# Full-width loads, one index load, one transpose of the token weights, and fillers moved to the known waits, in an attention and MLP kernel

## The chip, the cores and the metric

The kernel runs on 1 core of one Trainium2 chip. The metric is the device time of one execution in microseconds (us), the slowest core's, and with one core that is the only one. The kernel before took 499.61 us in the median of 3 runs (498.57 to 500.69).

## The reference, cut to what matters

Eight batches, each with 8 heads of 576 rows and head width 64, go through attention with a band of 32 rows to either side and 8 global rows and columns. An MLP block over 512 channels follows, which first mixes the 576 tokens with a 576x576 matrix.

```python
def _attn_ref(q, k, v, global_idx):               # (8, 8, 576, 64) each
    scores = scale * np.matmul(q, k.transpose(0, 1, 3, 2))
    mask = np.abs(pos[:, None] - pos[None, :]) <= 32
    mask = mask | is_global[:, None] | is_global[None, :]
    # ... softmax over the masked scores, then:
    return np.matmul(attn, v)

def _moe_ref(x, alpha1, beta1, w_tok, alpha2, beta2, w_ch1, w_ch2, lam):   # x is (8, 576, 512)
    a1 = alpha1 * x + beta1
    tok = np.einsum('ts,bsd->btd', w_tok, a1)     # token mixing
    u = x + lam * tok
    a2 = alpha2 * u + beta2
    ch = np.maximum(a2 @ w_ch1, 0.0) @ w_ch2      # the two large MLP matmuls
    return u + lam * ch
```

## The kernel before

The MLP matmuls of finished batches are a stock of independent work for TensorE. `front(b)` emits the attention and the token mixing of batch b and is a Python generator. Each `yield n` in it means "put n MLP matmuls here". These are the fillers: they keep TensorE busy while another engine prepares what attention needs next. There are none during batch 0, because the MLP has nothing to work on yet.

```python
for b in range(NB):
    for n in front(b):
        for _ in range(n):
            if b > 0:
                next(fill)                     # one MLP matmul of an earlier group
```

The loading phase, cut. `A(tile, offset, dims)` is an access pattern. `V`, `SC`, `G`, `T` are VectorE, ScalarE, GpSimd (POOL in the profile) and TensorE (PE). `nc.sync` is the queue of SyncE (SP).

```python
gbc_i = cp.tile([P, 8], I32, name="gbc_i")       # the global index on every partition: 128 x 8 pieces of 4 bytes
nc.scalar.dma_start(out=gbc_i, in_=bass.AP(gi32.tensor, gi32.offset, [[0, P], [2, 8]]))
# ... three more tiny loads of the same index
R = [cp.tile([P, 1536], FP32, name=f"R{i}") for i in range(3)]      # staging buffers

def load_qk(b):
    for hh in range(2):                           # k on 96 partitions, runs of 1536 bytes
        r = next_r()
        nc.sync.dma_start(out=A(r, 0, [[384, 4], [1, 384]], 0, PK), in_=k[b, 4 * hh : 4 * hh + 4, :, :].rearrange("h (p c) d -> p h (c d)", c=NK))
        (V if b == 0 else G).tensor_copy(...)     # cast to bf16
    for h0, nh in ((0, 3), (3, 3), (6, 2)):       # q on 72 partitions, runs of 2048 bytes
        ...
def load_v(b):
    ...                                           # v to ve, cast by POOL; vo is ve shifted by 64 rows:
    nc.sync.dma_start(out=A(vo, 0, [[1, 2080]], 0, 64), in_=A(ve, 0, [[1, 2080]], 64, 64))
    nc.sync.dma_start(out=A(vo, 0, [[1, 2080]], 64, 64), in_=A(ve, 520, [[1, 2080]], 0, 64))
```

One batch, cut to what the argument needs:

```python
def front(b):
    ...                                           # kqn: the gathered global rows of k and q, made by POOL
    for p in range(4):                            # four pairs of heads
        # 6 TensorE transposes of k; two VectorE copies of 64 x 576 from PSUM to KTz
        # 8 TensorE transposes of q; one ScalarE copy to QT
        # after p == 0: transpose of kqn, copies to KgT and QT
        yield 4
    ...
    def qk(p):                                    # scores of a head pair: 3 groups of 6 matmuls
        ...
        SC.activation(out=Pt[...], in_=ps[:, 0:432], func=AF.Exp, bias=0.0, scale=0.125)
        yield 4                                   # after each group
        ...                                       # VectorE makes GRT and PTz from Pt

    def pv(p):
        ...                                       # global rows: 10 matmuls on GRT, then VectorE copies to RS
        yield 4
        # values: matmuls of PTz with ve or vo, and one of RS for each block; VectorE makes x
        # POOL makes XL from x, the input of token mixing

    ...                                           # global scores: QT with KgT
    yield from qk(0)
    for p in range(4):
        if p < 3:
            yield from qk(p + 1)
        else:
            yield 4
        yield from pv(p)
    ...
    yield 14
    ...                                           # token mixing: 5 blocks of 5 matmuls on XL, yield 4 after each
```

KTz and QT hold the transposed k and q. kqn holds the gathered global rows of k and q, and KgT those of k, transposed. RS is what the global rows add to the values. LA1 is the product of alpha1 and lam, by which POOL scales x into XL. PSUM is the memory that TensorE writes into.

In the fillers' stream, `wt_prep(1)` stands before the first MLP matmul. It is a second preparation of the token weights (25 TensorE transposes, 10 small matmuls, the copies), for the odd batches, whose rows are shifted by 64.

The softmax here doesn't subtract the row's maximum and nothing guards it: scores larger than these inputs give would overflow.

## Time and profile before

I use the first global-score matmul of each batch, which reads `KgT`, as the mark between batches. It divides the 496.3 us of the profiled execution into five stages.

| stage (us from the start) | length | TensorE busy | idle |
|---|---|---|---|
| start to KgT of batch 0 (43.17) | 43.17 | 4.79 | 38.38 |
| to KgT of batch 1 (102.44) | 59.27 | 41.96 | 17.31 |
| batch 1 (to 152.83) | 50.39 | 45.89 | 4.50 |
| batches 2 to 6 (to 393.92) | 241.09 | 226.97 | 14.12 |
| batch 7 and the MLP tail (to 496.3) | 102.38 | 97.02 | 5.36 |

These are the lines behind it, the stage view of the kernel before. The columns are: window, length, then busy time and (number) of PE, PEld (weight loads), DVE (VectorE), ACT (ScalarE) and POOL, the granted clock of TensorE, the mean busy share of the DMA engines, and GB/s.

```profile
0.00:43.17 43.17, 4.79 (x57) 3.96 (x58) 20.38 (x61) 8.32 (x9) 25.60 (x35) 1.00 0.62 132
43.17:102.44 59.27, 41.96 (x486) 28.77 (x484) 39.12 (x76) 20.13 (x34) 34.66 (x37) 0.74 0.82 227
102.44:152.83 50.39, 45.89 (x465) 26.44 (x464) 26.64 (x54) 22.18 (x40) 24.05 (x25) 1.00 0.73 159
152.83:393.92 241.09, 226.97 (x2296) 130.56 (x2295) 127.17 (x263) 107.23 (x192) 88.83 (x93) 1.00 0.38 96
393.92:496.30 102.38, 97.02 (x648) 47.36 (x646) 25.05 (x51) 40.05 (x65) 6.88 (x8) 1.00 0.09 32
```

The first stage loads, TensorE hardly works in it, and the DMA engines are busy for only 0.62 of it. So neither limits it: something waits. In the second stage the clock column reads 0.74. TensorE had half its clock for three stretches of 10.24 us, 30.7 us in all. From 102 us on TensorE is nearly full, and its idle time is the question. The waits view names it. First the loading: the wait of the sync queue, then two lines of the queue's timeline (start, length, engine, line, what is issued).

```profile
SPq L167 <- DMA gbc_i<-in_global_idx_dram: 13.8, 1, 13.8
```

```profile
1.17 0.47 SPq L158 DMA_DIRECT2D R_102<-in_k_dram  x1
15.50 0.35 SPq L167 DMA_DIRECT2D R_103<-in_q_dram  x1
```

The queue issues k by 1.6 us and then stands still for 13.8 us before q. What it waits for is the landing of the index, in 1,024 pieces of 4 bytes. Later on TensorE waits for kqn, and POOL, which makes it, is held up by other work. The timeline of POOL in the kernel before, with the idle time before an instruction and its releaser in brackets:

```profile
25.20 1.26 POOL L503 TENSOR_TENSOR LA_240<-U,lamb 128x512 f32<-128x512 f32 x1 [9.16 <-DMA U<-in_moe_alpha_dram]
26.40 2.23 POOL L505 MEMSET XL_136<- 128x2560 bf16 x1
28.57 2.23 POOL L505 MEMSET XL_137<- 128x2560 bf16 x1
...
37.61 0.38 POOL L301 CAST kqn<-kq 64x128 bf16<-64x128 f32 x1
```

For the steady state, the waits of TensorE in the window of batches 2 to 6 alone, 152.83 to 393.92 us (total, times, longest):

```profile
PE sc L462 <- POOL XL_137 L412: 3.4, 2, 1.7
PE sc L462 <- POOL XL_136 L406: 2.6, 3, 0.9
PE xps L395 <- DVE RS_134 L382: 2.2, 6, 0.4
PE mm L316 <- DVE UT L452: 2.0, 5, 0.6
PE mm L316 <- DVE QT L324: 1.8, 3, 0.6
PE xps L395 <- DVE RS_133 L382: 1.1, 4, 0.6
```

Token mixing waits for XL: 6.0 us in five batches. The values wait for RS: 3.3 us. The transposes (L316) wait 3.8 us for VectorE to free a PSUM buffer. These 13.1 us are nearly all of the stage's 14.12 us of idle time.

### The profile page before, as it was taken

The numbers are of one execution on the slowest core, as the hardware profiler recorded it, in microseconds if no ns is written. First come the engines' busy times: TensorE is split into PE (matmuls) and PEld (weight loads), VectorE is DVE, ScalarE is ACT, GpSimd is POOL, SyncE is SP. The second block draws the span as 40 slices with busy tenths as digits, with TensorE's granted clock in tenths as the row PEclk, the third lists the DMA queues.
The fourth block names the chain that finished last, engine by engine and source line by source line (L and its number), as shares of the span: only waits on it lengthen the run. The fifth ranks groups of instructions, "written<-read, shape, count | busy, mean of one in ns | idle before, by whom it ended". The sixth has DMA issues, their size and how long they took to land. (4 is left out here: it accounts for less than half of the span.)

```text
span 496.3 us, 9426 instructions
## 1 busy us (share of the span) xinstructions
PE 416.6 (84%) x3942; PEld 237.1 (48%) x3942; DVE 238.4 (48%) x501; ACT 197.9 (40%) x337; POOL 180.0 (36%) x196
## 2 busy tenths in 40 slices
PE   0006767798899999998999999989999999999996
PEld 0004643455455555654556455545564555444442
DVE  4615756745464557353735472547354645501101
ACT  0225602185039503840384148214831581262440
POOL 4296495346606262426232543343233013000000
PEclk9999669699999999999999999999999999999999
DMA  4687767989766153706270645063103000101102
GB/s 95 160 153 200 259 167 231 222 198 191 164 146 150 45 136 92 190 4 163 66 187 20 151 108 143 24 143 86 35 22 87 23 1 22 44 21 42 44 5 81
DMA packets 62946, 53.60 MB, mean 108 GB/s; under 512 B 42088, under 2 KB 48616, under 8 KB 62904
## 3 DMA queue, kind: packets, MB, share of 16 engines
q1 hardware_dynamic: 59248, 51.73, 40.7%
q10 hardware_dynamic: 2888, 0.88, 0.9%
q0 software_dynamic: 768, 0.39, 0.4%
q8 instruction: 31, 0.51, 0.4%
q14 instruction: 11, 0.09, 0.1%
HBM read 39.30 MB, written 9.44 MB: 98 GB/s over the span
## 5 line engine op out<-in xcount | busy, mean ns | idle before, releaser
L485 PE MATMUL ml<-UT,W_139 128*128 128x512 bf16 x576 | 146.8, 379 | 0.0
L494 PE MATMUL ml<-W_140,HTb 128*128 128x512 bf16 x576 | 140.2, 379 | 0.0
L488 ACT ACTIVATE HTb<-ml,bias1T 128x512 bf16<-128x512 f32 x144 | 99.0, 687 | 43.0 <-PE ml L485 42.8
L494 PEld LDWEIGHTS <-HTb 128*128 128x128 bf16 x576 | 53.0, 98 | 55.6 <-issue 0.2
L485 PEld LDWEIGHTS <-W_139 128*128 128x128 bf16 x576 | 49.2, 98 | 41.8 <-issue 3.6
L351 ACT ACTIVATE Pt<-sc 128x432 f16<-128x432 f32 x96 | 50.4, 529 | 29.1 <-DVE rden L397 18.0
L498 DVE TENSOR_TENSOR U<-ml,U 128x512 f32<-128x512 f32 x36 | 24.9, 691 | 60.1 <-PE ml L494 59.8
L463 DVE TENSOR_TENSOR U<-sc,x 128x512 f32<-128x512 f32 (+1 forms) x40 | 27.6, 690 | 45.4 <-PE sc L462 45.4
L406 POOL TENSOR_TENSOR XL_137<-x,LA_240 128x512 bf16<-128x512 f32 x16 | 20.3, 1266 | 71.9 <-DVE x L399 71.9
L317 ACT COPY QT<-mm 128x576 bf16<-128x576 bf16 x32 | 20.4, 638 | 38.9 <-PE mm L316 38.9
L406 POOL TENSOR_TENSOR XL_136<-x,LA_240 128x512 bf16<-128x512 f32 x16 | 20.3, 1266 | 38.8 <-DVE x L399 38.7
L462 PE MATMUL sc<-XL_136,wtT_142 128*128 128x512 bf16 x100 | 26.1, 395 | 4.3 <-POOL XL_136 L406 4.3
L316 PE MATMUL mm<-identb,q_114 72*128 72x72 bf16 x256 | 14.5, 204 | 17.9 <-ACT q_114 L173 11.1
L462 PE MATMUL sc<-XL_137,wtT_143 128*128 128x512 bf16 x100 | 24.8, 379 | 5.3 <-POOL XL_137 L412 5.3
L399 DVE TENSOR_TENSOR x<-xps,rden 128x640 f32<-128x640 f32 x32 | 26.3, 823 | 1.4
L353 DVE TENSOR_TENSOR GRT_129<-Pt,grm 128x80 f16<-128x80 f16 x16 | 4.4, 277 | 42.6 <-ACT Pt L351 42.6
L308 PE MATMUL mm<-identb,k_115 96*128 96x96 bf16 x192 | 14.3, 214 | 11.0 <-DVE k_115 L162 9.5
L316 PEld LDWEIGHTS <-q_114 72*128 72x128 bf16 x256 | 12.5, 102 | 21.5 <-ACT q_114 L173 11.3
L300 POOL TENSOR_TENSOR kqn<-kq,cst 64x128 bf16<-64x128 f32 x8 | 3.2, 394 | 50.8 <-PE mm L321 50.8
L394 PEld LDWEIGHTS <-PTz_128 128*128 128x128 f16 x288 | 15.7, 100 | 10.4 <-issue 4.8
L394 PEld LDWEIGHTS <-PTz_127 128*128 128x128 f16 x288 | 15.8, 99 | 10.3 <-issue 7.9
L395 PE MATMUL xps<-RS_134,GS_132 128*128 128x65 f16 x160 | 15.7, 193 | 5.7 <-DVE RS_134 L382 5.4
(272 smaller groups left out, 698.5 us busy)
## 6 DMA issues: line engine op xcount, KB each, us to landing
out_dram<-U SPq DMA_DIRECT2D x36, 256.0 KB, 2.0
vo<-ve SPq DMA_DIRECT2D x16, 260.0 KB, 4.1
RV_105<-in_v_dram SPq DMA_DIRECT2D x16, 256.0 KB
R_101<-in_k_dram SPq DMA_DIRECT2D x6, 576.0 KB, 7.8
R_102<-in_k_dram SPq DMA_DIRECT2D x5, 576.0 KB, 5.7
R_103<-in_k_dram SPq DMA_DIRECT2D x5, 576.0 KB
R_103<-in_q_dram SPq DMA_DIRECT2D x6, 432.0 KB
R_101<-in_q_dram SPq DMA_DIRECT2D x5, 432.0 KB
```

The lines of the kernel that those rows point to most:

```text
L316: T.transpose(out=ps[:, c * PQ : (c + 1) * PQ], in_=q16[0:PQ, c, p * P : (p + 1) * P], identity=identb[0:PQ, 0:PQ])
L317: SC.copy(out=A(QT, 648 * p, [[72, 9], [8, 8], [1, 8]]), in_=A(ps, 0, [[8, 9], [1, 8], [PQ, 8]]))
L351: SC.activation(out=Pt[:, 432 * un : 432 * un + 432], in_=ps[:, 0:432], func=AF.Exp, bias=0.0, scale=0.125)
L394: T.matmul(out=o_, lhsT=ptz[:, base : base + P], rhs=vv, start=(i == 0), stop=False)
L399: V.tensor_tensor(out=A(x, P * p, [[64, 2], [DM, 5], [1, 64]]), in0=A(xps, 0, [[512, 2], [65, 5], [1, 64]]), in1=A(rden, 0, [[5, 2], [1, 5 ...
L406: G.tensor_tensor(out=A(xl, DM * full + P * p, [[DM, 4], [1, P]]), in0=A(x, DM * full + P * p, [[DM, 4], [1, P]]), in1=A(LA1, P * p, [[0, ...
L462: T.matmul(out=ps, lhsT=wtT[par][:, c, P * u : P * u + P], rhs=xl[:, c, :], start=(c == 0), stop=(c == 4))
L463: V.tensor_tensor(out=U[f][r0:r1, :], in0=ps[r0:r1, :], in1=x[r0:r1, u, :], op=ALU.add)
L485: T.matmul(out=ps, lhsT=W1[:, cc, ec * P : (ec + 1) * P], rhs=ut[:, cc, :], start=(cc == 0), stop=(cc == 3))
L488: SC.activation(out=HTb[:, slots[ec], :], in_=ps, func=AF.Relu, bias=bias1T[:, ec : ec + 1], scale=1.0)
L494: T.matmul(out=ps, lhsT=HTb[:, slots[ec], P * j : P * j + P], rhs=W2[:, ec, :], start=(ec == 0), stop=(ec == 15))
L498: V.tensor_tensor(out=u, in0=ps, in1=u, op=ALU.add)
```

## The change

Its intent has four parts.

1. **Loading.** The index comes in one load of 64-byte pieces and nothing slow stands ahead of q. k and q come on all 128 partitions in runs of 1 KB (rows 0 to 511), with a tail load of rows 512 to 575. POOL's memsets and LA1 are cut or moved.
2. **Transposes.** With 128 rows at a time, a head pair takes 4 + 4 transposes instead of 6 + 8, and the tails take 8 for all pairs: 41 a batch instead of 57, with the one for kqn.
3. **Token weights.** They are prepared once, and the odd batches' copy is made from it by two DMAs. The vo copies move from the sync queue to POOL's.
4. **Fillers.** They move from where nothing waits to where TensorE was seen waiting: before token mixing and between the global rows and the values.

```diff
-    R = [cp.tile([P, 1536], FP32, name=f"R{i}") for i in range(3)]
+    R = [cp.tile([P, 1024], FP32, name=f"R{i}") for i in range(4)]
...
-        nc.scalar.dma_start(out=gbc_i, in_=bass.AP(gi32.tensor, gi32.offset, [[0, P], [2, 8]]))
+    nc.scalar.dma_start(out=gi_t, in_=bass.AP(gi32.tensor, gi32.offset, [[0, P], [1, 16]]))
...
+        for i, src in enumerate((k, q)):
+            for hh in range(2):
+                r = next_r()
+                nc.sync.dma_start(
+                    out=A(r, 0, [[256, 4], [1, 256]]),
+                    in_=src[b, 4 * hh : 4 * hh + 4, 0:512, :].rearrange("h (p c) d -> p h (c d)", c=4),
+                )
...
-        nc.sync.dma_start(out=A(vo, 0, [[1, 2080]], 0, 64), in_=A(ve, 0, [[1, 2080]], 64, 64))
+        G.dma_start(out=A(vo, 0, [[1, 2080]], 0, 64), in_=A(ve, 0, [[1, 2080]], 64, 64))
... (the second vo copy likewise; the index arithmetic, now behind the first casts on VectorE)
-            for c in range(NK):
-                T.transpose(out=ps[:, c * PK : (c + 1) * PK], in_=k16[0:PK, c, p * P : (p + 1) * P], ...)
+            for c in range(4):
+                T.transpose(out=ps[:, c * P : (c + 1) * P], in_=kq16[:, 0, c, p * P : (p + 1) * P], identity=identb)
... (q likewise; then eight transposes of 64 rows for the tails)
                 SC.activation(out=Pt[:, 432 * un : 432 * un + 432], in_=ps[:, 0:432], func=AF.Exp, ...)
-                yield 4
+                yield 3
...
         for p in range(4):
             if p < 3:
-                yield from qk(p + 1)
+                nxt = qk(p + 1)
+                yield next(nxt) + 2
+                xg(p)                    # the global rows, once the first half of pv
+                yield 2
+                yield from nxt
             else:
-                yield 4
-            yield from pv(p)
+                yield 6
+                xg(p)
+                yield 6
+            pv(p)
+            yield 2
...
-        yield 14
+        yield 20
... (token mixing: yield 3 instead of 4 after each block)
+        nc.sync.dma_start(out=A(wtT[1], 64, [[640, 5], [1, S]], 64, 64), in_=A(wtT[0], 0, [[640, 5], [1, S]], 0, 64))
+        nc.sync.dma_start(out=A(wtT[1], 640 + 64, [[640, 4], [1, S]], 0, 64), in_=A(wtT[0], 0, [[640, 4], [1, S]], 64, 64))
...
     def filler():
         bias1()
-        wt_prep(1)
```

## The prediction

> **What bounds the kernel now.** From the first global-score matmul of batch 1 (KgT, 102.4 us in the PE timeline) to the end (496.3) TensorE is the limit: the stage table has it busy 235.8 of 250 us between 150 and 400, then comes a 57 us tail of MLP matmuls 213 ns apart. Batches follow every 50.3 and 46.7 us in turn, 48.5 on average. The idle 5.6 us per pair of batches is a short list: token mixing waits for POOL's scaled x (1.68 and 0.88), the global-row matmul for RS (0.32 to 0.57, about three a pair), q transposes for PSUM (0.6 each). Before 102.4 us the kernel loads: TensorE is busy 2.8 us of the first 40.
>
> The q load is not bandwidth bound: the sync queue stands still from 1.6 to 15.5 us. The instruction order shows why: it reuses a DMA semaphore (eight in turn) whose last user, the index broadcast in 1,024 four-byte pieces, lands near 15. Then POOL, in order, waits 9.2 us for alpha1/lam, spends 4.5 us on XL memsets and waits for v before it makes kqn (37.2-38.0), for which the second transpose group waited 16 us. KgT of batch 0 starts at 43.2. Later, 87-96 us is the second token-weight preparation (mixed with W2 scaling on DVE) before the first MLP matmul at 96.4.
>
> **What the change does.**
> - Index: 128 64-byte pieces; nothing slow ahead of q. k and q (2.36 MB) stream at once. With 1 KB runs at about 250 GB/s (estimate between the trace's rates for 256 B and 4 KB packets), q lands near 10 us, tails near 13.
> - hg_idx now stands on DVE behind the tail cast: 13.5 us (7.8 before). Gathers take 4 us to issue, 5 to land: kqn near 25, then two copy groups: KgT of batch 0 near 30, 13 us earlier.
> - Attention of batch 0 keeps its 22 us. The second weight preparation goes (two SBUF copies by DMA, off the path), 8 us. W2 scalings still sit between KTz copies of batch 1, and v(1) queues behind W2. KgT of batch 1 near 80: 22 us gained.
> - Per batch, 57 transposes become 41: per head pair 0.70 us of TensorE becomes 0.44, plus 0.35 for tails: 0.7 us a batch, 5 in all.
> - Fillers moved: 22 matmuls (4.7 us) before token mixing instead of 14 (3.0), which covers the 1.68 wait; RS is made eight fillers ahead of use. About 1.5 us a batch, 10 in all.
>
> Sum: 22+5+10 = 37 of 499.6.
>
> **Prediction: 463 us, 8 in 10 between 450 and 478.** Faster by over 2%: 0.95; within: 0.04; slower: 0.01.
>
> **What would show it.** KgT of batch 0 at 28-33 and of batch 1 at 77-84; q landing by 12; batch period 46 instead of 48.5; no POOL wait before token mixing; tail near 57.
>
> **What would make it wrong.** ve/vo of batch 1 late (behind W2, then POOL's DMA), stalling values past 88; gathers slow under a full queue; ACT limiting the score stage with three fillers a group (exp 0.47 + 3/4 of a 0.59 relu against 0.84 on TensorE); half clock: three 10 us stretches lie in 48-97 us. The Trainium skill ("TensorE: Matmul & The Clock Gate", Part 1) says idleness throttles the clock; the trace agrees in that they follow the idle phase; the same number is assumed.

## The result, and the profile after

The changed kernel is correct and takes **471.0 us** in the median of 4 runs (468.55 to 471.4). The kernel before took 500.15 us in the runs beside it (498.57 to 500.81). The ratio is 0.9411, with a 95% interval of 0.9371 to 0.9452. The prediction was 463 us, with 450 to 478 as its range: the total came out inside it, 8 us above the centre. (The profiled executions are 26.9 us apart, 496.3 and 469.4 us, and the medians 29.1.)

The stage view of the kernel after, with the same marks and columns as before:

```profile
0.00:32.90 32.90, 4.62 (x42) 3.64 (x42) 15.52 (x39) 5.51 (x7) 15.33 (x30) 1.00 0.89 240
32.90:87.08 54.18, 38.38 (x435) 27.09 (x434) 41.29 (x79) 20.81 (x36) 41.59 (x43) 0.78 0.63 187
87.08:141.91 54.83, 48.13 (x449) 27.34 (x447) 27.26 (x59) 22.36 (x41) 28.26 (x33) 0.94 0.84 199
141.91:369.96 228.05, 223.51 (x2218) 128.22 (x2217) 125.57 (x273) 107.12 (x197) 84.53 (x102) 1.00 0.35 97
369.96:469.40 99.44, 95.43 (x643) 46.61 (x641) 24.45 (x51) 39.20 (x65) 6.88 (x8) 1.00 0.09 32
```

Line by line against the view before, each stage's gain is the difference of the two lengths:

| stage | before | after | gain | predicted |
|---|---|---|---|---|
| start to KgT of batch 0 | 43.17 | 32.90 | 10.3 | 13 |
| to KgT of batch 1 | 59.27 | 54.18 | 5.1 | 9 |
| batch 1 | 50.39 | 54.83 | -4.4 | about 2 |
| batches 2 to 6 | 241.09 | 228.05 | 13.0 | about 11 |
| batch 7 and tail | 102.38 | 99.44 | 2.9 | the rest |
| sum | 496.3 | 469.4 | 26.9 | 37 |

The predicted column splits the 37 us of the prediction by stage: its 15 us for transposes and fillers are about 2.2 a batch. The loading phase gave less than predicted, the steady state somewhat more, and batch 1 became slower. Half-rate clock takes 30.7 us in both kernels, so its amount does not explain the total. Its place moved, though: 6.83 us of it now lie in batch 1 (clock 0.94 instead of 1.00).

The loading after: the sync queue's longest wait, then its timeline, then POOL's timeline around kqn.

```profile
SPq L531 <- DVE GRT_109 L337: 16.5, 1, 16.5
```

```profile
1.23 0.49 SPq L139 DMA_DIRECT2D R_95<-in_k_dram  x1
1.77 0.50 SPq L139 DMA_DIRECT2D R_96<-in_q_dram  x1
...
45.91 0.33 SPq L531 DMA_DIRECT2D R_95<-in_moe_w_ch_dram  x1
```

```profile
16.61 1.12 POOL L174 DMA_INDIRECT kq<-in_k_dram,hg_idx  x1 [8.71 <-DVE hg_idx L190]
...
29.62 0.29 POOL L280 CAST kqn<-kq 64x128 bf16<-64x128 f32 x1 [6.62 <-DMA kq<-in_k_dram,hg_idx]
```

q is now issued at 1.77 us instead of 15.50. But the gathers are now issued at 16.61, because the index arithmetic stands on VectorE behind the last cast of the tails; before, the first gather was issued at 8.24. Then POOL waits 6.62 us for a gather to land. A new standstill has also appeared on the sync queue. The MLP weights (L531) pass through four staging buffers, whose casts stand on VectorE and ScalarE behind attention work, so the fifth of these loads is issued at 45.91, 16.5 us late by the waits view.

TensorE's waits in batches 2 to 6 of the kernel after, all but two of 0.2 us:

```profile
PE mm L297 <- DVE KTz L299: 2.5, 5, 0.6
PE ml L478 <- DVE U L491: 1.7, 3, 0.6
```

The waits for XL and RS are gone, as intended. In their place, half a microsecond a batch is lost at the new transposes, which wait for VectorE's copies to KTz to free their PSUM buffers. In the whole execution three waits stand out that the kernel before did not have, or had shorter (its longest for x is 2.1 us). The waits view of TensorE in the kernel after:

```profile
PE xps L380 <- DVE x L385: 5.9, 3, 3.8
PE xps L380 <- DMA vo<-ve: 4.6, 1, 4.6
PE mm L358 <- DVE GRT_108 L337: 4.1, 1, 4.1
```

All of these fall ahead of KgT of batch 2: the list of the window above has none of them. The one for vo, at 101.6 us, stands in the stage that became slower. The stage view there, in slices of 2 us:

```profile
98.00:100.00 2.00, 0.00 (x0) 0.00 (x0) 0.00 (x0) 0.00 (x0) 1.03 (x1) 1.00 1.09 283
100.00:102.00 2.00, 0.37 (x7) 0.37 (x8) 0.00 (x0) 0.00 (x0) 1.04 (x1) 0.63 1.09 272
102.00:104.00 2.00, 2.00 (x27) 1.45 (x25) 0.58 (x3) 0.00 (x0) 0.00 (x0) 0.50 1.25 233
```

TensorE stops at 97.0, resumes at 101.6, and its clock falls to half at 100.5, inside the wait. All the while the DMA engines are full (share about 1). The clock then stays at half for 6.83 us.

### The profile page after: what moved, and what is told of

Read it like the earlier page. It is cut to its first block, busy times and chain, and to the rows that moved or that the text cites. A ratio compares the mean times of both kernels' runs of the same rounds, so it can differ in the third digit from the quotient of the medians.

```text
span 469.4 us, 9110 instructions
## 1 busy us (share of the span) xinstructions
PE 410.1 (87%) x3779; PEld 232.9 (50%) x3779; DVE 234.1 (50%) x497; ACT 195.0 (42%) x344; POOL 176.6 (38%) x213
## 3 DMA queue, kind: packets, MB, share of 16 engines
q0 software_dynamic: 2048, 4.66, 4.5%
## 4 chain that ended last, share of the span: by engine, by line
PE 75%; POOL 7%; DMA 7%; DVE 6%; issue 3%; SPq 0%; ACT 0%; POOLq 0%; DVEq 0%; ACTq 0%
PE ml L487 26%; PE ml L478 24%; PE sc L455 8%; PE xps L380 4%; PE sc L328 4%; PE mm L358 3%; DVE KTz L299 3%; PE xps L381 2%; DMA vo<-ve 2%; DMA kq<-in_k_dram,hg_idx 2%; DMA R_94<-in_k_dram 1%; PE mm L443 1%; DMA R_94<-in_q_dram 1%; PE sc L410 1%; POOL W_119 L542 1%
## 5 line engine op out<-in xcount | busy, mean ns | idle before, releaser
L478 PE MATMUL ml<-UT,W_118 128*128 128x512 bf16 x576 | 155.4, 386 | 1.7 <-DVE U L491 1.7
L299 DVE COPY KTz<-mm 64x512 bf16<-64x512 bf16 x64 | 44.0, 687 | 1.5 <-PE mm L297 0.3
L328 PEld LDWEIGHTS <-KTz 128*128 128x128 bf16 x576 | 32.2, 103 | 22.1 <-issue 3.1
L328 PE MATMUL sc<-QT,KTz 128*128 128x72 bf16 x576 | 36.0, 204 | 0.6 <-ACT Pt L335 0.5
L303 ACT COPY QT<-sc 128x512 bf16<-128x512 bf16 x32 | 18.6, 584 | 41.4 <-PE sc L302 40.8
L455 PE MATMUL sc<-XL_116,wtT_122 128*128 128x512 bf16 x100 | 24.8, 379 | 0.0
L455 PE MATMUL sc<-XL_115,wtT_121 128*128 128x512 bf16 x100 | 24.7, 379 | 0.0
L297 PE MATMUL mm<-identb,kq_101 128*128 128x128 bf16 x128 | 13.8, 237 | 12.0 <-DVE kq_101 L147 8.5
L380 PEld LDWEIGHTS <-PTz_106 128*128 128x128 f16 x288 | 16.9, 104 | 8.6 <-DMA vo<-ve 4.8
L380 PE MATMUL xps<-ve,PTz_107 128*128 128x65 f16 x160 | 16.6, 197 | 5.1 <-DVE x L385 5.1
L380 PE MATMUL xps<-vo,PTz_106 128*128 128x65 f16 x128 | 16.2, 203 | 4.6 <-DMA vo<-ve 4.6
```

The source lines that it names most:

```text
L299: V.tensor_copy(out=A(KTz, 640 * (2 * p + hh) + 32, [[4, P], [1, 4]], 64 * hh, 64), in_=A(ps, 0, [[1, P], [P, 4]], 64 * hh, 64))
L328: T.matmul(out=ps[:, i * 144 + 72 * hh : i * 144 + 72 * hh + 72], lhsT=KTz[:, 2 * p + hh, 64 * t : 64 * t + P], rhs=QT[:, p, 72 * t : 72 * ...
L380: T.matmul(out=o_, lhsT=ptz[:, base : base + P], rhs=vv, start=(i == 0), stop=False)
L455: T.matmul(out=ps, lhsT=wtT[par][:, c, P * u : P * u + P], rhs=xl[:, c, :], start=(c == 0), stop=(c == 4))
L478: T.matmul(out=ps, lhsT=W1[:, cc, ec * P : (ec + 1) * P], rhs=ut[:, cc, :], start=(cc == 0), stop=(cc == 3))
```

## The experiments

Twelve kernels ran on three chips. The median of the kernel before was 499.24, 499.9 and 496.8 us on them, so runs are compared by their ratio to the kernel before. I held that the four terms of the prediction are real and about the size it gave them (theory A); its rivals (theory B in most of the quoted texts) say that another wait already holds the same time, so that a part alone gives little. Each text says what it meant in its run.

| run | from | median us | ratio to before (95%) |
|---|---|---|---|
| e1, index alone | before | 493.13 | 0.988 (0.9856 to 0.9905) |
| e2, fillers alone | before | 479.74 | 0.9611 (0.9574 to 0.9647) |
| e3, old fillers | after | 488.98 | 0.9802 (0.9781 to 0.9822) |
| e6, index arithmetic first | after | 467.64 | 0.9386 (0.934 to 0.9432) |
| e4, vo on the sync queue | after | 464.29 | 0.9286 (0.926 to 0.9311) |
| e5, token weights twice | after | 469.68 | 0.9396 (0.9369 to 0.9424) |
| e9, tail copies on ScalarE | after | 471.98 | 0.9428 (0.9404 to 0.9453) |
| e10, v ahead of W2 | after | 463.17 | 0.9265 (0.9239 to 0.9292) |
| e12, two KTz copies on ScalarE | after | 466.59 | 0.9396 (0.9358 to 0.9433) |
| e13, token mixing's fillers alone | before | 486.47 | 0.9787 (0.9752 to 0.9822) |
| c1, combination | after | 462.37 | 0.929 (0.9255 to 0.9326) |
| c2, combination with e12 | after | 457.38 | 0.9209 (0.917 to 0.9248) |

All gave the reference's result. The marks, in us from the start of each profiled execution:

| run | KgT of batch 0 | of batch 1 | of batch 2 | batches 2 to 6 |
|---|---|---|---|---|
| before | 43.17 | 102.44 | 152.83 | 241.09 |
| e1 | 40.66 | 98.25 | 147.69 | 241.40 |
| e2 | 42.94 | 104.48 | 150.39 | 228.34 |
| e13 | 42.84 | 100.87 | 148.32 | 234.70 |
| e3 | 31.25 | 92.65 | 142.56 | 243.11 |
| after | 32.90 | 87.08 | 141.91 | 228.05 |
| e6 | 26.16 | 91.91 | 138.34 | 228.04 |
| e4 | 32.03 | 88.49 | 135.89 | 228.04 |
| e5 | 32.06 | 91.52 | 138.37 | 228.04 |
| e9 | 31.80 | 87.84 | 144.14 | 229.12 |
| e10 | 31.94 | 82.57 | 133.54 | 228.04 |
| e12 | 31.89 | 85.80 | 138.43 | 226.31 |
| c1 | 29.64 | 79.99 | 133.86 | 228.04 |
| c2 | 28.82 | 74.44 | 128.60 | 226.29 |

This table carries much of the argument. The fillers and the transposes of the changed kernel fix the fourth column to 228.04 or 228.05, whatever loading does; only e9 and e12, which move copies of the transposes, change it. So what loading is worth is read at KgT of batch 2, and not earlier: a gain at the first or second mark can be given back by the third.

### e2: the fillers alone

```diff
-                yield 4
+                yield 3
... (in the before kernel: xg split from pv, the fillers around it, 20 before token mixing,
...  3 in it, as in the change; loading and transposes as before)
```

> The kernel before with only the filler matmuls moved (3 instead of 4 behind each exp, global rows made eight fillers ahead of their use, 22 instead of 14 before token mixing). Theory A (the moved fillers close the known waits): TensorE idle in the five middle batches falls from 14.1 us to about 5, the run gains 9 to 13 us on before. Rival B (the idle fell because transposes and copies got fewer or shorter): gain under 4 us.

Measured: 479.74 us, a gain of 19.5 us, where the prediction had 10 for fillers. The stage view of e2, batch 1 and then batches 2 to 6:

```profile
104.48:150.39 45.91, 45.22 (x465) 26.18 (x463) 26.93 (x54) 21.91 (x40) 24.32 (x25) 1.00 0.79 174
150.39:378.73 228.34, 223.94 (x2297) 129.69 (x2295) 125.67 (x263) 106.70 (x192) 88.67 (x93) 1.00 0.40 102
```

And all of TensorE's waits in its batches 2 to 6:

```profile
PE mm L316 <- DVE UT L461: 2.0, 5, 0.6
PE mm L316 <- DVE QT L324: 1.8, 3, 0.6
```

The waits for XL and RS are gone, 9.3 us, and the waits at the transposes stay as they were, to the tenth. The idle time falls from 14.12 to 4.40. The busy time falls too, from 226.97 to 223.94, although the same matmuls run but for one. Of these 3.0 us, 2.7 lie in the values' matmuls, the ones that wait for RS (tile xps: busy 23.30 us before, 20.62 in e2). So "busy" here is not pure work; it fits that matmuls which are pending behind a wait count in part. The Trainium skill ("Perfetto Trace Analysis", "Identifying the Most-Contended Engine") says that matmul busy time is not a good measure of how close a kernel is to its limit, because pipelined matmuls look smaller in the trace. The measure errs too, but by showing too much: 3.0 of the 12.75 us that this stage gained were hidden in the busy column. The prediction had counted idle waits only.

### e13: the fillers of token mixing alone

```diff
-        yield 14
+        yield 22
...
-            yield 4
+            yield 3
...
-            yield 8
+            yield 5
```

> The kernel before with only the fillers ahead of token mixing raised from 14 to 22, taken from the token mixing stage and the last wait; score stage, global rows and values untouched. Splits the 19.5 us that all the moved fillers gained. Theory A (token mixing's wait for POOL, 1.68 and 0.88 us, is a part, the RS and exp waits of the score and values stages the rest): gain 6 to 10 us. Rival B (token mixing's wait is nearly all of it): gain above 15 us. Rival C (the gain is in the score and values stages alone): gain under 3 us.

Measured: a ratio of 0.9787, a gain of 10.3 us by the medians. In batches 2 to 6 the wait for XL is gone, and the largest that remains is this line of e13's waits (against 2.2 + 1.1 before):

```profile
PE xps L395 <- DVE RS L382: 2.9, 10, 0.6
```

So half of the fillers' worth comes from token mixing and the other half from the new places around the global rows and the scores.

### e3: the changed kernel with the old fillers

```diff
-                yield 3
+                yield 4
... (xg put back into pv, 14 before token mixing, 4 in it: the fillers of before)
```

> The kernel after with the old filler places. Theory A (fillers and loading add up independently): 9 to 13 us slower than after, so about 481 us. Rival B (the new transposes and copies already removed the waits): under 4 us slower, below 475 us.

Measured: 488.98 us, a gain of 10.3 us over before. The KgT mark of batch 2 is 10.3 us earlier than before, and batches 2 to 6 take 243.11 us, 2.0 us *more* than before. The gains of e2 and e3 add to 29.8 us against 29.1 for the whole change: the two halves are independent. But e3 shows two misses of the prediction at once. Loading is worth 10.3 us, not 22, and the transposes are worth nothing. With the old fillers they cost 2.0 us in five batches, and with the new ones (after against e2) they gain 0.3 us. (Both comparisons hold everything else that the change alters within a batch as well, such as the vo copies on POOL's queue.) With the old fillers TensorE's waits for RS grew from 3.3 to 6.2 us in these batches and those for XL stayed at 6.0:

```profile
PE xps L379 <- DVE RS L366: 6.2, 13, 0.7
PE mm L297 <- DVE KTz L299: 3.8, 5, 0.9
PE sc L446 <- POOL XL L396: 3.4, 2, 1.7
PE sc L446 <- POOL XL L390: 2.6, 3, 0.9
```

### Why the transposes gave nothing: e9 and e12

The groups of VectorE's copies from the transposes, first two of the eight such groups of the kernel before (the others differ by at most 0.01 us a copy from one or the other), then both groups of the kernel after. The columns are operation, shapes and count, then busy us and mean ns, then idle before.

```profile
L310 DVE COPY KTz_121<-mm 64x576 bf16<-64x576 bf16 x8 | 6.1, 761 | 0.1
...
L310 DVE COPY KTz_122<-mm 64x576 bf16<-64x576 bf16 x8 | 6.0, 749 | 1.2 <-PE mm L308 0.6
```

```profile
L299 DVE COPY KTz<-mm 64x512 bf16<-64x512 bf16 x64 | 44.0, 687 | 1.5 <-PE mm L297 0.3
L312 DVE COPY KTz<-mm 64x256 bf16<-64x256 bf16 x16 | 4.6, 289 | 0.8 <-PE ml L478 0.3
```

Fewer transposes did not mean fewer copies. A batch has 8 copies of about 0.755 us before, which is 6.0 us of VectorE, and 8 of 0.687 and 2 of 0.289 after, which is 6.1 us. From the first transpose of a batch to its KgT, VectorE is busy 7.10 of 7.42 us before and 7.08 of 7.34 after (batch 6 in both). The stage after holds 20 fillers where the one before held 18, so the lengths do not compare like with like. TensorE did save something: all its transposes in batches 2 to 6 (those with `identb`) are busy 25.51 us before and 23.08 after, 0.49 us a batch. But its whole busy time falls by only 0.43 us in the five batches (e2 to after). The prediction counted TensorE's saving, 0.7 us a batch, in a stage that VectorE fills as well.

e9 moved the two tail copies to ScalarE:

```diff
-            V.tensor_copy(out=A(KTz, 640 * hh + 544, [[1280, 4], [1, 64]], 64 * hh, 64), ...)
+            SC.copy(out=A(KTz, 640 * hh + 544, [[1280, 4], [1, 64]], 64 * hh, 64), ...)
```

> The kernel after with the two KTz tail copies of each batch (64 x 256) on ScalarE instead of VectorE, nothing else. Theory A (the transpose stage, 7.35 and 7.94 us in turn, is bound by VectorE's PSUM copies, which is why 17 fewer transposes gained nothing): the stage becomes 0.4 to 0.7 us shorter in each of batches 2 to 7, the run 2.5 to 5 us shorter. Rival B (TensorE or ScalarE binds the stage): stage and run unchanged within 1 us, or longer because ScalarE delays the exps.

Measured: 471.98 us, no gain. The stage is unchanged at 7.35 us (even batches) and 7.94 (odd), and batches 2 to 6 take 1.1 us more. This test was not decisive. The tails come last in the stage, after the copy that frees the last PSUM buffer, so moving them takes nothing from what TensorE waits for.

e12 moved two of the eight large copies, which lie in the middle of the stage:

```diff
-                V.tensor_copy(out=A(KTz, 640 * (2 * p + hh) + 32, ...), ...)
+                (SC.copy if hh == 1 and p in (0, 2) else V.tensor_copy)(out=A(KTz, 640 * (2 * p + hh) + 32, ...), ...)
```

> The kernel after with two of the eight KTz copies of each batch (second half of head pairs 0 and 2, 64 x 512) on ScalarE instead of VectorE. The run with the tail copies moved did not test VectorE's bound, because those stand after the last copy that frees PSUM for the transposes. Theory A (VectorE, busy 7.08 of 7.34 us, binds the transpose stage): in the even batches the stage falls from 7.35 to 6.6-6.9 us, the run 2.5 to 5 us shorter than after (or 2 to 4 us if ScalarE delays a relu). Rival B (TensorE's own work or ScalarE binds it): stage within 0.2 us of 7.35 and run unchanged within 1.5 us.

Measured: the stage shortens to 7.12 and 7.51 us, and batches 2 to 6 from 228.05 to 226.31, 0.35 us a batch. By ratio the whole run cannot be told from the kernel after (0.9396 against 0.9411, intervals that overlap). The wait for KTz in batches 2 to 6, 2.5 us in the kernel after, is now:

```profile
PE mm L297 <- DVE KTz L299: 1.0, 3, 0.3
```

So VectorE does bind the stage, but only in part: releasing it returns 1.7 us in five batches (about 2.8 in eight, an estimate from this figure) of the 5 that were predicted for the whole, and the stage lands between the two theories. The trace says what holds it now: TensorE is busy 6.94 of the 7.12 us of an even batch (6.78 of 7.34 in the kernel after), so hardly any idle time is left there. How much of this busy time is work is not shown.

### e1: the index alone

```diff
-    gbc_i = cp.tile([P, 8], I32, name="gbc_i")
... (and the other tiny loads of the index)
+    nc.scalar.dma_start(out=gi_t, in_=bass.AP(gi32.tensor, gi32.offset, [[0, P], [1, 16]]))
+    nc.scalar.dma_start(out=cst, in_=nc.inline_tensor(_consts(), name="cst_np").ap())
... (the index arithmetic of the change, ahead of everything else on VectorE)
```

> The kernel before with one part of the change alone: one index load of 128 runs of 64 bytes in place of the four-byte pieces, index arithmetic on VectorE as in the kernel after; loads, transposes, fillers, weight preparation stay. Theory A (the index broadcast holds a DMA semaphore that the second q load has to wait for, and so everything queued behind it): the second q load is issued by 5 us instead of 15.5, KgT of batch 0 comes at 30 to 35 us instead of 43.2, and the run is 6 to 12 us shorter than before. Rival B (POOL's order, LA1, memsets and v before kqn, binds by itself): KgT of batch 0 stays above 40 us and the run gains under 3 us.

Measured: a gain of 6.1 us (ratio 0.988), but neither theory holds as written. q is issued at 9.74 us and not by 5. The sync queue still waits, now for the load of the constants, which q does not use either:

```profile
SPq L169 <- DMA cst<-cst_np: 8.1, 1, 8.1
```

The packed traces keep the numbers of the semaphores, which the views leave out. They show the cause that the prediction inferred: the loads of the sync and scalar queues use eight numbers in turn (100 and 102 to 108), and q's first load waits for the number that it shares with that earlier load, 104 with the index before and 103 with the constants in e1.

kqn is ready at 31.5 us instead of 38.0. From its first gather at 11.56 to kqn POOL never waits more than 0.3 us, so there its order (LA1, memsets and v before kqn) does set the time. But KgT of batch 0 comes only 2.5 us earlier, at 40.66: between kqn and KgT lie 9.1 us instead of 5.2, because VectorE, still busy with constants, copies to KgT only at 34.64, and TensorE then waits three more times. So q's blockage was real, and behind it stood POOL's order and then VectorE's. That is why the change had to move POOL's work as well.

This run also gives a hint of what the clock is worth here. Its half-rate stretches come to 6.83 us against 30.7 before, and yet its stage from KgT of batch 0 to that of batch 1 is 57.59 us against 59.27. So most of the half rate in that stage seems to hide behind other waits; as other waits moved too, this is not a measurement of it.

### e6: the index arithmetic first

```diff
+    V.tensor_copy(out=gbc, in_=A(gi_t, 0, [[2, 8]]))
+    V.tensor_tensor(out=gtmp, in0=gbc, in1=cst[:, C_OH : C_OH + 8], op=ALU.mult)
... (the sum and hg_idx too: moved ahead of the casts of batch 0)
```

> The kernel after with the gather index computed first on VectorE, ahead of the k/q tail cast, so POOL's gathers start near 6 us instead of 16.6. Theory A (the late index delays kqn and with it batch 0): KgT of batch 0 at 22 to 27 us instead of 32.9, KgT of batch 1 5 to 9 us earlier than 87.1, run 4 to 9 us shorter than after. Rival B (batch 0 and batch 1 are paced by later arrivals and casts, W1, W2, POOL's LA1): KgT of batch 0 earlier, but KgT of batch 1 within 2 us of 87 and the run within 2 us of after.

Measured: KgT of batch 0 comes 6.7 us earlier than after, at 26.16, but KgT of batch 1 comes at 91.91, 4.8 us *later*. At the third mark 3.6 us of the gain are left, and by ratio the run cannot be told from after (0.9386 against 0.9411, intervals that overlap). Most of the time was lost at one wait, in e6's timeline of TensorE:

```profile
44.48 0.73 PE L360 MATMUL mm<-ve,GRT 128*128 128x65 f16 x10 [11.93 <-DVE GRT L339]
```

GRT waits on VectorE behind the constants that need a row of column numbers (the iota). The kernel before loads it; the change makes it on POOL, where it comes in this order behind eight gathers, at 35.1 us. The wait was 4.1 us in the kernel after and ended at 42.63; here it is 11.9 us and ends at 44.48. So all of the 6.7 us is gone there, and 1.9 more; where the other 3.0 us up to KgT of batch 1 went is not settled. In c1, where the iota also goes first, TensorE's list has no wait for GRT any more. So this link is shown.

### e5: the token weights prepared twice again

```diff
-            wt_prep()
+            wt_prep(0)
... (the second preparation back in the filler stream, no DMA copies)
         bias1()
+        wt_prep(1)
```

> The kernel after with the token weights of the odd batches prepared as before, by a second round of 25 transposes and 10 matmuls on TensorE ahead of the first MLP matmul, in place of the two SBUF copies. Theory A (this preparation sits on the path of batch 1, as predicted, 8 us): KgT of batch 1 6 to 9 us later than 87.1, run 5 to 9 us longer than after. Rival B (the phase is paced by the arrival and scaling of the weights and of v, so the removed work was covered): KgT of batch 2 within 3 us of 141.9 and run less than 3 us longer.

Measured: 469.68 us, by ratio no slower than after. KgT of batch 1 does come 4.4 us later, but KgT of batch 2 comes 3.5 us *earlier*, because batch 1 has no wait for vo. The second preparation, worth 8 us in the prediction, is worth nothing in this kernel: what it saves is spent again at the next wait.

### e4 and e10: the wait for vo

```diff
-        G.dma_start(out=A(vo, 0, [[1, 2080]], 0, 64), in_=A(ve, 0, [[1, 2080]], 64, 64))
+        (G if b == 0 else nc.sync).dma_start(out=A(vo, 0, [[1, 2080]], 0, 64), in_=A(ve, 0, [[1, 2080]], 64, 64))
... (the second copy likewise)
```

> The kernel after with the vo copies of batches 1 to 7 issued by the sync queue again (batch 0 stays on POOL); the compiled order then has vo of batch 1 ahead of the k and q loads of batch 2. Theory A (the 4.64 us wait of batch 1 comes from vo sharing the DMA rings with those 2 MB, from its place in the traffic): the wait for vo at the first values matmuls of batch 1 falls below 1.5 us, KgT of batch 2 comes 3 to 5 us before 141.9, run 3 to 5 us shorter unless later batches wait more. Rival B (v of batch 1 itself is late): wait stays above 3 us and the run stays within 1.5 us of after.

Measured: 464.29 us. The wait is gone, batch 1 takes 47.40 us instead of 54.83, and its clock is 1.00. The time from issue to landing of the vo copies tells why (minimum, median, maximum in us), first in the kernel after, then in e4:

```profile
DMA to landing us min/median/max: 2.9/5.5/8.9
```

```profile
DMA to landing us min/median/max: 2.8/2.9/2.9
```

In e4 the copies of batch 1 are issued 2.1 and 1.2 us *later*, at 93.59 and 94.20, because the sync queue waits for ve first, and they land earlier. In the kernel after they were issued at 91.46 and 92.96, and their packets ran until 100.74 among 2.10 MB of k and q of batch 2, which the sync queue had issued from 89.81 on. On the sync queue, k and q come behind vo (from 95.52). The Trainium skill ("DMA: Bandwidth & Descriptors", "Queues, rings and completion order") says that a DMA engine takes turns between its queues packet by packet; the interleaved packets fit that, but no run separates the change of queue from the change of order. POOL's queue is not slow by itself: in batch 0 of the kernel after, where no other load runs beside them, the first of its vo copies lands 2.9 us after its issue.

The other way to mend it leaves vo on POOL's queue and moves the load of v ahead of that of W2:

```diff
-                w2_load()
             load_v(b + 1)
+            if b == 0:
+                w2_load()
```

> The kernel after with the loads of v of batch 1 issued ahead of those of W2 on the sync queue. Theory A (the wait of 4.64 us for vo in batch 1 is the end of the chain W1, k/q, W2, v through one queue and four staging buffers): the vo wait is gone, KgT of batch 2 3 to 5 us earlier, run 3 to 5 us shorter. Rival B (W2, now 4 us later, holds up VectorE's W2 scalings and with them KTz and KgT of batch 1): KgT of batch 1 3 us or more later, run within 1.5 us of after.

Measured: 463.17 us. The wait for vo is gone here too, and KgT of batch 1 comes at 82.57, 4.5 us earlier than after, because VectorE's W2 scalings (four of 1.2 us in after) no longer stand among the KTz copies; the half-rate stretch of 6.83 us that begins there at 76.64 us in after is gone too. But batch 1 still takes 50.97 us: the scalings have moved into it (VectorE is busy 36.26 us there, 27.26 after), and token mixing waits 2.01 us for XL.

One more regularity shows in these runs. Three kernels have a wait for vo in batch 1: after (4.64 us), e9 (6.37) and e12 (2.85). In each, the clock falls to half inside that wait, 3.5, 4.3 and 2.0 us after it began, and stays there for 6.83 us. In e4, e5, e6 and e10, which have no such wait (e6 has one of 0.38), batch 1 runs at full clock. But it is not the wait for vo as such: c1 and c2 (below) have none, and in their batch 1 a half-rate stretch of 3.41 us begins at the end of a wait of 2.26 us for RS (c1) and 1.2 us after the end of one of 2.30 us for XL (c2). The loss of 7.4 us in batch 1 of after against e4 divides into 4.3 us of idle time (6.70 against 2.43) and 3.2 us of longer busy time (48.13 against 44.97). The second part fits work done at half rate: the wait cost more than its own length.

### c1 and c2: combinations

c1 has e10's order, e6's index arithmetic and the iota first on POOL. c2 adds e12's copies on ScalarE. The diffs are those shown above, and the line of the iota moved ahead of the loads.

> The kernel after with three changes that the runs point to: gather index first on VectorE, iota for the global rows first on POOL, v of batch 1 ahead of W2 on the sync queue. If they add up: KgT of batch 0 near 26 us, no wait for iota in batch 0 (4.1 us in after, 11.9 with the index alone), KgT of batch 1 near 77 us, KgT of batch 2 near 126, run 455 to 460 us. If something else paces the loads (four staging buffers recycled by casts that stand behind attention work on VectorE and ScalarE): KgT of batch 1 not before 81 and the run 460 to 464.

Measured: 462.37 us, no better than e10 alone (ratios 0.929 and 0.9265). KgT of batch 1 comes at 79.99, 2.6 us earlier than in e10, and by KgT of batch 2 the difference is gone (133.86 against 133.54). The pieces do not add up.

> The combined kernel with two KTz copies of each batch on ScalarE as well. If VectorE binds the transpose stage: 2.5 to 5 us shorter than the combined kernel alone. If not: within 1.5 us of it.

Measured: **457.38 us**, a ratio of 0.9209, the fastest: 5.0 us below c1 on the same chip in the median, and below both kernels by ratio. The profiled executions of c1 and c2 are 7.0 us apart (461.3 and 454.3): 1.75 us of it are in batches 2 to 6, and 5.3 us are there by KgT of batch 2. Its stage view, batch 1:

```profile
74.44:128.60 54.16, 47.79 (x448) 26.35 (x447) 36.20 (x59) 22.62 (x43) 30.19 (x32) 0.97 0.84 220
```

What paces the kernel until KgT of batch 2 once vo is mended stays open. Batch 1 still takes 54 us here against 45 later. The candidates are the four staging buffers, VectorE with the W2 scalings (busy 36.20 of 54.16 us), and the DMA engines (share 0.84). The kernel with six staging buffers did not fit in SBUF, and so did not run.

## Why the prediction was right or wrong

The total was right, and so was the direction of nearly every part. But its sum, 22 + 5 + 10, held because one term was too small and two were too large. Measured, the terms are about 10 + 0 + 19.5.

- **Fillers, predicted 10 us: the right mechanism, the wrong size.** e2 measured 19.5 alone, and e13 shows that half of it is token mixing. The term was sized from the idle waits in the list, about 1.5 us a batch. Two things were missed. Part of the wait is inside the busy time (3.0 us in batches 2 to 6 of e2), and the gain also falls in batch 1 (4.5 us: 50.39 to 45.91) and in the last stage (2.1 us), where the waits were not counted.
- **Batch period and signs.** "46 instead of 48.5" for the period: 45.6 (228.05 over five) against 48.2 before. "No POOL wait before token mixing": right. Tail: nearly unchanged, as said (from the first token-mixing matmul of batch 7 to the end 73.5 us before and 71.4 after).
- **Transposes, predicted 5 us: wrong.** The failed step is "per head pair 0.70 us of TensorE becomes 0.44": a saving on an engine that was not the only limit there. TensorE's transposes did save 0.49 us a batch, but VectorE's copies fill the stage too, and they stayed at 6 us a batch. e12 recovers 0.35 us a batch by taking load from VectorE; then TensorE is busy in nearly the whole stage.
- **Loading, predicted 22 us at KgT of batch 1: too large.** It was 15.4 there and 10.9 at the next mark, and e3 measures 10.3 for loading in the finished time. Within it:
  - KgT of batch 0 came at 32.9, at the late edge of "28-33". q landed at 13.85 instead of 10, hg_idx came at 16.2 instead of 13.5, and kqn waited 6.62 us for a gather.
  - "The second weight preparation goes, 8 us": it moved KgT of batch 1 by 4.4 us (e5), and none of this reached the end.
  - "KgT of batch 1 near 80": it came at 87.08. e6 and c1 show one of the waits in between, the one for the iota; e10 shows the W2 scalings as another.
- **The wait for vo.** "What would make it wrong" named it: vo of batch 1 late on POOL's DMA. It happened, and cost about 6 us in the finished time (e4 by its profiled span, 463.5 against 469.4). It should have been a term of the sum and not only a warning.
- **Clock.** "The same number is assumed": 30.7 us of half rate in both. But the number was luck. e1 and e3 have 6.83 us, and it matters where the stretch falls: in batch 0 it seems to have cost little (e1), and behind the wait for vo it came on top.

## What to carry to other kernels

A saving counts only as far as no other engine fills the same stage: count what the change leaves on the others before you take credit for fewer instructions on one. Read a gain in loading at the first mark where the kernel has settled, since here gains of several microseconds at the first two marks were given back by the third. And when a copy moves to another DMA queue, ask what is already queued beside it at that moment, because a transfer that is issued earlier can land later.

## What the Trainium skill lacked or had wrong

- "TensorE: Matmul & The Clock Gate", Part 1, names a window of 3,413 ns, and the traces agree: every half-rate stretch in the traces, but for the one cut off by the end of the execution, is a whole number of 3.413 us (3.41 to 17.07). But the rule in "Why this matters for your kernels", "No PE-idle gaps >~3µs between matmul bursts", was not safe here: in e12 the clock fell to half 2.0 us into a wait of 2.85 us, and stayed there for 6.83 us. TensorE had been busy for 1.40 of the 3.41 us before.
- "DMA: Bandwidth & Descriptors", "Specifications", gives 512 bytes as the smallest transfer for full rate. In the first 150 us of the kernel after, the median packet of 256 bytes took 18 ns (14 bytes a ns and engine), of 1,024 bytes 46 ns (22), of 2,048 bytes 84 ns (24) and of 4,096 bytes 159 ns (26). So the rate still rose above 512 bytes; no packet had just 512.
- I found no page that warns of a queue standing still because a DMA semaphore's earlier user has not landed. Here a load in 1,024 pieces of 4 bytes held the sync queue for 13.8 us, and in e1 the load of the constants held it for 8.1 us, each through the semaphore number that it shares with q's load (104 and 103 in the traces).
